# RWKV attention and a SoLU MLP on one core: v of the second half rounded by its own load, issued on GpSimd

## The chip, the core and the metric

The kernel runs on one core of one Trainium2 chip. The core's engines are PE (TensorE: matrix products and transposes), DVE (VectorE), ACT (ScalarE), POOL (GpSimd) and SP (SyncE, which here only issues transfers); 16 DMA engines move data between memory and the core's buffers. The metric is device time in microseconds (us), the median of several runs.

## What is computed

For 4 batches, 8 heads, 768 steps and heads of 48 numbers, a recurrence with a decaying state; the result is laid out as 3072 rows of 384 and goes through an MLP with a softmax gate and a normalization. Cut to what matters:

```python
for t in range(S):
    cur = np.einsum('bhd,bhe->bhde', u[None] * kt, vt)
    y[:, :, t] = np.einsum('bhd,bhde->bhe', rt, state + cur)
    state = wt[:, :, :, None] * state + np.einsum('bhd,bhe->bhde', kt, vt)
...
h = x @ w_in
e = np.exp(h - h_max)
solu = h * (e / np.sum(e))
ln = (solu - mean) / np.sqrt(var + 1e-06) * g_ln
out = ln @ w_out
```

r, k, v and w come in float32 as (batch, head, step, 48).

## The kernel before

The work is cut into 24 units: 6 chunks of 128 steps by 4 batches; unit i is chunk i // 4 of batch i % 4. In a unit the 128 steps lie on the 128 partitions and the 8 heads of 48 numbers side by side. Each unit passes through some forty small stages. The order of all stages of all units is one long string of words, `ORDER` (lines 21 to 66), that a loop at the end reads from left to right (lines 555 to 558): the word `vb12.p` calls the stage `vb` for unit 12 with the choice `p`. Each engine takes its own instructions strictly in that order (class `InOrder`, lines 71 to 89; this is why the profile gives line 85 for nearly all of them, and why groups are told apart by their tiles). An engine that has to wait for one instruction holds back all that it has behind it. Choices behind the dot are an engine (`a` ACT, `d` DVE, `p` POOL, `t` a transpose by DMA) or a bank of the PE's accumulators.

The stages that the change and the steps of the prediction touch:

- Loads `LW`, `LK`, `LR`, `LV` (lines 245 to 255): SP issues one transfer each for w, k, r and v of a unit. A unit's tile is 128 partitions by 8 heads by 48 numbers; in memory each run of 48 float32 stands alone, so a transfer is 1024 pieces of 192 bytes, 192 KB in all. The targets are rings of NIO = 7 tiles.
- `vb` (`v_cast`, line 355): a copy of v from float32 to bf16, on ACT, DVE or POOL as the word says, into one of NLW = 10 tiles `vb_t`.
- `p`, `q`, `qh` (POOL), `dg` (DVE), `dv` (`bonus_v`, POOL): the bonus term. p is r times k, q is p times u, `qh` adds the halves of q for some units, dg sums over a head, and dv is `vb` times dg.
- `S` (PE, line 433): the state's update, which reads kp and `vb`. `Y` (PE, line 405): the attention output, which reads the masked scores m and `vb`. `y` (ACT or DVE) brings it out; on DVE it adds dv.
- `M`, `m`, `sel`: the scores, their copy out (with the mask, on DVE; without it, on ACT) and the mask on POOL for those copied by ACT.
- The MLP: `X`, `xT` (transpose of y, two units by DMA), `H` (PE), `e` (ACT), `he` (DVE), `ea` (POOL, for 16 units, adds the halves of e), `hq` (ACT or DVE), `Oa`, `Ob` (PE), `sq`, `lv` (ACT), `qm` (DVE), `o` (ACT or DVE) and `out` (a store issued by SP).

The casts of v of units 12 to 23 stand on POOL for units 12, 13, 15, 16, 17, 18, 21 and 23, on DVE for 14, and on ACT for 19, 20 and 22. The word `LV` of these units stands 1 to 24 words before its `vb`.

SP has an in-order queue too. A load there waits until the tile that it overwrites has been read, and each transfer waits for the one eight before it to have landed.

Of the kernel before, what the change touches and what calls it, by code (L numbers as in the profile page):

```python
# [34 lines left out]
ex10 Oa2.3 st4 kr7.d dg7 LR9 LK9 kp9 X5.7 xT5.a LR10 Ob2 sq2 p9 q9 LK10 kp10 p10 cum11.6 ex11 qm2 lv2 o2.a S7.2  # L35
M7.4 m7.d H5.0 LK11 LR11 kp11 et7 st7 e5 he5 hq5.d dv7 out1 out3 LV9 vb9.d krk10.3 krr10 kr10.a p11 q11 Y7.n5
y7.d krk11.4 H6.6 ea5.p e6 M10.2 krr11 m10.a ea6.p qh9 LW12 lw12 krk9.1 krr9 LK12 LW15 lw15 kr9.d Oa5.0 X7.5
xT7.a he6 LR12 p12 out2 LK15 Ob5 sq5 dg9 q12 q10 qh12 kr11.d LR15 LV8 S9.1 et9 vb8.p sel10 st9 qm5 cum15.2 ex15
kp15 hq6.a cum12.6 ex12 kp12 H7.4 e7 he7 Oa4.1 LV12 qh11 vb12.p LV10 vb10.p LV11 dv8 M9.2 m9.a vb11.p sel9 Ob4
sq4 qm4 lv5 S8.7 hq7.d et8 st8 LW14 krk12.6 krr12 dg10 Y8.n3 y8.d kr12.a Oa6.2 lv4 o5.a M11.4 m11.a dg12 M12.6  # L40
m12.d Ob6 sq6 qm6 S10.0 et10 st10 S12.3 lv6 X8.5 xT8.d LK13 dv10 Y10.n4 y10.d o4.d et12 LW13 lw13 lw14 o6.a st12
S11.7 et11 st11 LR14 LR13 Oa7.6 LK14 dg11 LV13 cum13.4 ex13 kp13 cum14.0 ex14 kp14 H8.2 e8 dv12 Y12.i7 y12.a
X10.5 xT10.d dv9 p15 Y9.i4 y9.a sel11 LW18 lw18 LW16 krk14.1 krr14 vb13.p S13.0 et13 he8 lw16 dv11 p13 q13 hq8.a
LK16 H10.4 e10 X12.7 kr14.d M14.2 m14.a LW17 lw17 xT12.d dg13 X9.1 xT9.d st13 Y11.n7 y11.d p14 q14 Ob7 cum16.0
ex16 cum18.2 ex18 sq7 Oa8.7 he10 LR16 p16 q16 hq10.a kp16 qm7 lv7 X11.5 ea10.p sel14 LR18 LK18 kp18 Ob8 sq8
xT11.d qm8 cum17.0 ex17 krk13.4 krr13 o7.a kr13.d qh14 out4 LR17 LK17 kp17 H9.2 lv8 M13.4 m13.d LV16 e9 krk16.6
krr16 kr16.a H11.0 e11 q15 dg14 qh15 vb16.p S16.5 Oa10.4 LV14 vb14.d dv14 S14.6 o8.d he9 he11 krk17.7 krr17
kr17.d et16 Ob10 sq10 qm10 et14 hq9.a lv10 out5 out6 LV15 dv13 ea11.p p18 p17 LK19 st16 dg15 st14 out7 LW19 lw19
H12.2 e12 Y13.n1 Y14.n0 M17.6 y13.d X13.5 xT13.a o10.d Oa9.1 y14.d m17.a vb15.p q18 ea12.p cum19.4 ex19 Ob9 sq9
dg16 he12 qm9 lv9 q17 o9.a LR19 kp19 p19 dv15 sel17 X14.0 xT14.d H13.6 e13 M16.2 dv16 q19 qh19 m16.a sel16  # L50
hq11.d kr15.t M15.4 m15.d he13 H14.0 e14 ea13.p hq12.a LW20 lw20 qh18 ea14.p Oa11.5 kr18.t LV17 Y15.n4 y15.d
Ob11 he14 hq13.a sq11 out8 out10 M18.2 S15.7 et15 dg17 vb17.p LV18 out9 qm11 lv11 X15.6 xT15.a LR20 m18.d Oa12.4
cum20.0 ex20 st15 Ob12 sq12 qm12 Y16.n6 y16.d H15.2 o11.a LK20 LW21 kp20 vb18.p p20 dg18 dv18 dv17 X16.7 xT16.d
lv12 o12.d Y17.n5 e15 he15 lw21 hq14.a dg19 S17.6 et17 st17 y17.d H16.0 e16 q20 Y18.n7 Oa14.4 cum21.2 LW22 lw22
ex21 Ob14 sq14 y18.d he16 X18.6 xT18.a Oa13.5 kr19.t M19.0 LR21 LK21 ea15.p p21 q21 ea16.p hq16.a hq15.a kr20.t
kp21 LR22 m19.d M20.6 m20.d out12 H18.2 e18 ea18.p he18 LK22 p22 q22 Ob13 cum22.0 X17.7 xT17.a sq13 qm13 qm14
Oa16.6 ex22 kp22 LW23 lw23 lv13 o13.d hq18.d S18.7 et18 st18 dg20 LV19 vb19.a LK23 Ob16 sq16 qm16 dv19 LR23 LV20
lv14 o14.a H17.2 e17 he17 Oa15.1 cum23.4 ex23 ea17.p vb20.a dv20 qh21 Oa18.0 lv16 o16.a p23 q23 kp23 Y19.n7
y19.d Ob18 sq18 hq17.a Ob15 sq15 Y20.n3 y20.d X19.2 xT19.a kr21.t M21.4 m21.a sel21 dg22 dg21 qm18 kr22.t M22.6
m22.d qm15 S19.3 Oa17.2 et19 st19 LV22 vb22.a dv22 H19.4 out14 out11 lv18 o18.d lv15 o15.a Y22.n7 e19 Ob17 sq17  # L60
y22.d X22.6 dg23 qm17 lv17 xT22.a out13 o17.a he19 hq19.a LV21 vb21.p dv21 Y21.n3 xT20.t H20.0 e20 y21.d ea19.p
kr23.t M23.6 m23.d H22.4 e22 he20 hq20.a Oa19.2 LV23 vb23.p dv23 Y23.n3 y23.d out18 out16 he22 xT21.t H21.6 e21
X23.1 ea20.p hq22.d Ob19 sq19 xT23.a qm19 out17 he21 out15 lv19 o19.a out19 Oa20.0 hq21.d H23.4 e23 ea22.p Ob20
sq20 qm20 lv20 he23 hq23.d o20.a out20 ea21.p Oa21.3 Oa22.1 Ob21 sq21 qm21 lv21 Ob22 sq22 o21.a out21 qm22 lv22
o22.d out22 ea23.p Oa23.7 Ob23 sq23 qm23 lv23 o23.a out23
"""

NIO, NLW, NKP, NWK = 7, 10, 6, 4
# [24 lines left out]
def kernel(  # L93
# [25 lines left out]
    pe, act, dve, pool, sp = (InOrder(tc, e) for e in (nc.tensor, nc.scalar, nc.vector, nc.gpsimd, nc.sync))  # L119
# [6 lines left out]
    def ring(name, n, shape, dtype):  # L126
        return [consts.tile(shape, dtype, name=f"{name}{j}") for j in range(n)]
# [69 lines left out]
    vb_t = ring("vb", NLW, [C, H, D], BF16)  # L197
# [43 lines left out]
    def rows_of(src, i):  # L241
        c, b = units[i]
        return src[b, :, c * C:(c + 1) * C, :].rearrange("h t d -> t h d")
# [101 lines left out]
    def bonus_half(i, x):  # L345
        q = q_t[i % 3]
        pool.tensor_add(out=q[:, :, :D // 2], in0=q[:, :, :D // 2], in1=q[:, :, D // 2:])

    def v_cast(i, x):
        copy = {"a": act.copy, "d": dve.tensor_copy, "p": pool.tensor_copy}[x]  # L350
        copy(out=vb_t[i % NLW], in_=v_t[i % NIO][:, :, :D])
# [189 lines left out]
    def store(i, x):  # L541
# [4 lines left out]
        ih=make_halves, ik=make_keep, LW=load_w, LK=load_k, LR=load_r, LV=load_v, LU=load_u, LG=load_g, LI=load_w_in, LO=load_w_out,  # L546
        us=spread_u, uc=copy_u, gs=turn_g, gc=copy_g, wi=cast_w_in, gw=gain, mn=column_mean, mc=copy_mean,
        ce=centre, hot=warm_up,
        lw=log_w, cum=cumulate, ex=decays, kp=scaled, p=bonus_rk, q=bonus_u, vb=v_cast, dg=bonus_sum, qh=bonus_half, dv=bonus_v,
        krk=transposed_k, krr=transposed_r, kr=transposed_copy, M=scores, m=scores_copy, sel=scores_mask,  # L550
        Y=attend, y=y_copy, S=state, et=state_decay, st=state_update, X=x_transposed, xT=x_copy,
        H=hidden, e=hidden_exp, he=hidden_mul, ea=hidden_add, hq=hidden_square, Oa=output_a, Ob=output_b,
# [36 lines left out]
```

## Time and profile before

| | |
|---|---|
| median of 3 runs | 151.62 us (149.74 to 153.84) |
| the profiled execution | 152.17 us; its span 150.4 us |
| busy PE / DVE / ACT / POOL | 134.1 / 121.4 / 120.6 / 117.6 us |
| transfers of SP's queue | 113026 packets, 28.79 MB, 88.1% of the time of 16 DMA engines |
| loads of v | 24 of 192 KB, 3.8 us from issue to landing at the median |
| casts of v | 18 on POOL (9.4 us), 3 on DVE (1.4 us), 3 on ACT (1.5 us) |
| granted clock of PE | 1.0 |

The span is the time from the first to the last instruction of the profiled execution. A line of groups reads: source line, engine, operation, written tile `<-` read tiles, partitions x numbers and type, how many, then busy us and mean ns of one, then the idle time of the engine just before them and what ended it. A line of waits reads: who waited for whom, us in total, how many times, the longest. A line of the chain of work that ended last reads: start, length, engine and tile.

### The profile page before, as it was taken

To read this page: it belongs to the slowest core of one execution; us is meant where nothing else is said; L and a number is where in the kernel's file an instruction comes from. 1 tells how busy PE (TensorE), PEld (TensorE's weight loads), DVE (VectorE), ACT (ScalarE), POOL (GpSimd) and SP (SyncE) were. 2 spreads that over 40 slices of the span, in tenths; PEclk is the share of its full clock that TensorE was granted. 3 is DMA by queue.
4 is the path that set the end of the run, shared out by engine and by line. 5 is a ranking of instruction groups with operands and counts; after the bars stand their busy time and mean duration, and the time that the engine had idled before them with its cause. 6 is when DMAs were issued, how large, how long until landed. Compare 5 with 4: busy or idle time off the path is not lost.

```text
span 150.4 us, 5113 instructions
## 1 busy us (share of the span) xinstructions
PE 134.1 (89%) x2047; PEld 101.9 (68%) x2047; DVE 121.4 (81%) x216; ACT 120.6 (80%) x245; POOL 117.6 (78%) x152
## 2 busy tenths in 40 slices
PE   6967779788989999999999999989999999979960
PEld 2323548486667779777797889777977878868630
DVE  5025985799978999978997999999998989796620
ACT  3159588989987997999699995998898999986670
POOL 7339794897959999699989999999996989693300
PEclk9999999999999999999999999999999999999999
DMA  4999999599989999997999998998999996850131
GB/s 99 215 214 196 293 386 316 106 221 210 192 159 245 183 256 197 219 220 152 195 203 202 228 264 187 171 236 190 193 153 263 153 242 156 192 170 0 57 144 68
DMA packets 113051, 29.11 MB, mean 194 GB/s; under 512 B 108538, under 2 KB 112643, under 8 KB 113027
## 3 DMA queue, kind: packets, MB, share of 16 engines
q1 hardware_dynamic: 113026, 28.79, 88.1%
q8 instruction: 16, 0.26, 0.7%
q14 instruction: 9, 0.07, 0.2%
HBM read 22.03 MB, written 4.72 MB: 178 GB/s over the span
## 4 chain that ended last, share of the span: by engine, by line
PE 32%; POOL 13%; DVE 13%; DMA 12%; SPq 11%; ACT 11%; issue 5%; POOLq 0%
PE ps L85 32%; SPq L85 11%; DMA wout_f<-in_moe_w_out_dram 7%; POOL q L85 3%; DVE he L85 3%; POOL dv L85 3%; DMA xT<-y 3%; POOL p L85 3%; DMA kr_in<-in_r_dram 3%; POOL m L85 2%; DVE w L85 2%; POOL vb L85 2%; DVE kp L85 2%; ACT o L85 2%; DVE m L85 2%
## 5 line engine op out<-in xcount | busy, mean ns | idle before, releaser
L85 PE MATMUL ps<-w,he 128*128 128x385 bf16 x192 | 44.4, 324 | 0.5 <-DVE m L85 0.5
L85 PE MATMUL ps<-xT,win_sb 128*128 128x128 bf16 x576 | 36.0, 219 | 1.1 <-DMA xT<-y 1.1
L85 PEld LDWEIGHTS <-win_sb 128*128 128x128 bf16 x576 | 32.7, 98 | 2.7 <-issue 1.2
L85 PE MATMUL ps<-one_col,hq 128*128 128x1 bf16 x192 | 31.5, 164 | 0.0
L85 DVE TENSOR_TENSOR he<-ps,e 128x1024 bf16<-128x1024 f32 x24 | 29.1, 1218 | 0.6 <-ACT e L85 0.4
L85 DVE TENSOR_TENSOR kp<-ps,kr_in 128x768 bf16<-128x768 f32 x24 | 22.5, 951 | 8.4 <-ACT ps L85 7.5
L85 POOL TENSOR_TENSOR p<-kr_in 128x384 bf16<-128x384 f32 x24 | 24.0, 1001 | 6.0 <-DMA kr_in<-in_r_dram 5.0
L85 ACT ACTIVATE e<-ps 128x1024 bf16<-128x1024 f32 x24 | 24.5, 1019 | 5.1 <-PE ps L85 4.3
L85 POOL TENSOR_TENSOR ea<-e 128x512 bf16<-128x512 bf16 x16 | 18.4, 1154 | 7.3 <-ACT sq L85 4.2
L85 POOL TENSOR_TENSOR dv<-vb,dg 128x384 bf16<-128x384 bf16 x24 | 20.8, 876 | 2.7 <-DVE qm L85 1.7
L85 POOL TENSOR_TENSOR q<-p,u_bc 128x384 bf16<-128x384 bf16 x24 | 21.8, 912 | 1.2
L85 PEld LDWEIGHTS <-hq 128*128 128x128 bf16 x192 | 15.6, 96 | 8.5
L85 PEld LDWEIGHTS <-he 128*128 128x128 bf16 x192 | 18.4, 96 | 3.4
L85 ACT ACTIVATE ps<-ps 128x768 f32<-128x768 f32 x24 | 18.9, 800 | 0.7 <-PE ps L85 0.7
L85 DVE TENSOR_TENSOR m<-ps,keep 128x1024 bf16<-128x1024 f32 x14 | 17.0, 1218 | 1.3 <-PE ps L85 1.3
L85 PEld LDWEIGHTS <-kp 128*128 128x128 bf16 x216 | 13.1, 97 | 4.3 <-DVE kp L85 1.8
L85 ACT ACTIVATE hq<-he 128x1024 bf16<-128x1024 bf16 x15 | 15.7, 1055 | 0.1
L85 ACT ACTIVATE lw<-w_in 128x384 bf16<-128x384 f32 x23 | 11.8, 522 | 1.8 <-DMA w_in<-in_w_dram 1.8
L85 DVE TENSOR_REDUCE dg<-q 128x8 f32<-128x384 bf16 (+1 forms) x24 | 10.8, 453 | 2.2 <-POOL q L85 2.2
L85 PEld LDWEIGHTS <-kr 64*128 64x128 bf16 (+1 forms) x272 | 10.1, 95 | 3.6 <-ACT kr L85 1.2
L85 PE MATMUL ps<-ident,kp 128*128 128x128 bf16 x136 | 10.5, 220 | 1.7 <-DVE kp L85 1.2
L85 POOL CAST vb<-v_in 128x384 bf16<-128x384 f32 x18 | 9.4, 531 | 3.0 <-DMA v_in<-in_v_dram 3.0
(88 smaller groups left out, 289.8 us busy)
## 6 DMA issues: line engine op xcount, KB each, us to landing
kr_in<-in_k_dram SPq DMA_DIRECT2D x24, 192.0 KB, 3.8
kr_in<-in_r_dram SPq DMA_DIRECT2D x24, 192.0 KB, 4.0
w_in<-in_w_dram SPq DMA_DIRECT2D x24, 192.0 KB, 3.7
v_in<-in_v_dram SPq DMA_DIRECT2D x24, 192.0 KB, 3.8
out_dram<-o SPq DMA_DIRECT2D x24, 192.0 KB, 3.0
win_f<-in_moe_w_in_dram SPq DMA_DIRECT2D x3, 512.0 KB, 5.9
wout_f<-in_moe_w_out_dram SPq DMA_DIRECT2D x2, 768.0 KB, 9.8
kr<-kp SPq DMA_TRANSPOSE x7, 4.1
```

Source lines behind the costliest of these rows:

```text
L85: made = make(*args, **kwargs)
```

## The change

For units 12 to 23 the SP load of v into a float32 tile and the cast into `vb_t` are gone. In their place a transfer issued on POOL writes `vb_t` directly; it reads float32 and rounds to bf16 on the way. 24 words leave `ORDER` (`LV12` to `LV23` and `vb12` to `vb23`) and 12 come (`VB12` to `VB23`); all others keep their order. On POOL the twelve stand in this way (by the profile before, the place in front of each ends at the time in parentheses):

- `VB12` behind qh of unit 12 (66.6 us), `VB13` behind the mask of unit 9 (72.4)
- `VB16`, `VB14` behind q of unit 13 (80.4), `VB15` behind qh of unit 15 (88.6)
- `VB18` behind dv of unit 16 (101.3), `VB17` behind q of unit 19 (102.2), `VB19`, `VB20` behind q of unit 20 (110.9)
- `VB22` behind q of unit 22 (119.5), `VB21` behind qh of unit 21 (123.7), `VB23` behind q of unit 23 (125.7)

From each, 54 to 57 words of `ORDER` lie before the first stage that reads that tile. They wait for nothing else than their place: the tile was last used ten units earlier.

```diff
-xT7.a he6 LR12 p12 out2 LK15 Ob5 sq5 dg9 q12 q10 qh12 kr11.d LR15 LV8 S9.1 et9 vb8.p sel10 st9 qm5 cum15.2 ex15
-kp15 hq6.a cum12.6 ex12 kp12 H7.4 e7 he7 Oa4.1 LV12 qh11 vb12.p LV10 vb10.p LV11 dv8 M9.2 m9.a vb11.p sel9 Ob4
+xT7.a he6 LR12 p12 out2 LK15 Ob5 sq5 dg9 q12 q10 qh12 kr11.d LR15 LV8 VB12 S9.1 et9 vb8.p sel10 st9 qm5 cum15.2
+ex15 kp15 hq6.a cum12.6 ex12 kp12 H7.4 e7 he7 Oa4.1 qh11 LV10 vb10.p LV11 dv8 M9.2 m9.a vb11.p sel9 Ob4 sq4 qm4
...
+    def load_v_rounded(i, x):
+        pool.dma_start(out=vb_t[i % NLW], in_=rows_of(v, i))
+
     def v_cast(i, x):
         copy = {"a": act.copy, "d": dve.tensor_copy, "p": pool.tensor_copy}[x]
         copy(out=vb_t[i % NLW], in_=v_t[i % NIO][:, :, :D])
...
-        lw=log_w, cum=cumulate, ex=decays, kp=scaled, p=bonus_rk, q=bonus_u, vb=v_cast, dg=bonus_sum, qh=bonus_half, dv=bonus_v,
+        lw=log_w, cum=cumulate, ex=decays, kp=scaled, p=bonus_rk, q=bonus_u, vb=v_cast, VB=load_v_rounded, dg=bonus_sum, qh=bonus_half, dv=bonus_v,
```

More of the change, by code (lines that the diff above doesn't have):

```diff
@@ L37 @@
 y7.d krk11.4 H6.6 ea5.p e6 M10.2 krr11 m10.a ea6.p qh9 LW12 lw12 krk9.1 krr9 LK12 LW15 lw15 kr9.d Oa5.0 X7.5
-xT7.a he6 LR12 p12 out2 LK15 Ob5 sq5 dg9 q12 q10 qh12 kr11.d LR15 LV8 S9.1 et9 vb8.p sel10 st9 qm5 cum15.2 ex15
-kp15 hq6.a cum12.6 ex12 kp12 H7.4 e7 he7 Oa4.1 LV12 qh11 vb12.p LV10 vb10.p LV11 dv8 M9.2 m9.a vb11.p sel9 Ob4
-sq4 qm4 lv5 S8.7 hq7.d et8 st8 LW14 krk12.6 krr12 dg10 Y8.n3 y8.d kr12.a Oa6.2 lv4 o5.a M11.4 m11.a dg12 M12.6
+xT7.a he6 LR12 p12 out2 LK15 Ob5 sq5 dg9 q12 q10 qh12 kr11.d LR15 LV8 VB12 S9.1 et9 vb8.p sel10 st9 qm5 cum15.2
@@ L41 @@
+ex15 kp15 hq6.a cum12.6 ex12 kp12 H7.4 e7 he7 Oa4.1 qh11 LV10 vb10.p LV11 dv8 M9.2 m9.a vb11.p sel9 Ob4 sq4 qm4
+lv5 S8.7 hq7.d et8 st8 LW14 krk12.6 krr12 dg10 Y8.n3 y8.d kr12.a Oa6.2 lv4 o5.a M11.4 m11.a VB13 dg12 M12.6
 m12.d Ob6 sq6 qm6 S10.0 et10 st10 S12.3 lv6 X8.5 xT8.d LK13 dv10 Y10.n4 y10.d o4.d et12 LW13 lw13 lw14 o6.a st12
-S11.7 et11 st11 LR14 LR13 Oa7.6 LK14 dg11 LV13 cum13.4 ex13 kp13 cum14.0 ex14 kp14 H8.2 e8 dv12 Y12.i7 y12.a
-X10.5 xT10.d dv9 p15 Y9.i4 y9.a sel11 LW18 lw18 LW16 krk14.1 krr14 vb13.p S13.0 et13 he8 lw16 dv11 p13 q13 hq8.a
@@ L44 @@
-LK16 H10.4 e10 X12.7 kr14.d M14.2 m14.a LW17 lw17 xT12.d dg13 X9.1 xT9.d st13 Y11.n7 y11.d p14 q14 Ob7 cum16.0
+S11.7 et11 st11 LR14 LR13 Oa7.6 LK14 dg11 cum13.4 ex13 kp13 cum14.0 ex14 kp14 H8.2 e8 dv12 Y12.i7 y12.a X10.5
+xT10.d dv9 p15 Y9.i4 y9.a sel11 LW18 lw18 LW16 krk14.1 krr14 S13.0 et13 he8 lw16 dv11 p13 q13 hq8.a LK16 H10.4
+e10 X12.7 kr14.d M14.2 m14.a LW17 lw17 xT12.d dg13 X9.1 xT9.d VB16 st13 Y11.n7 VB14 y11.d p14 q14 Ob7 cum16.0
 ex16 cum18.2 ex18 sq7 Oa8.7 he10 LR16 p16 q16 hq10.a kp16 qm7 lv7 X11.5 ea10.p sel14 LR18 LK18 kp18 Ob8 sq8
-xT11.d qm8 cum17.0 ex17 krk13.4 krr13 o7.a kr13.d qh14 out4 LR17 LK17 kp17 H9.2 lv8 M13.4 m13.d LV16 e9 krk16.6
@@ L47 @@
[L47 to L65, printed above, removed]
+xT11.d qm8 cum17.0 ex17 krk13.4 krr13 o7.a kr13.d qh14 out4 LR17 LK17 kp17 H9.2 lv8 M13.4 m13.d e9 krk16.6 krr16
@@ new lines @@
+kr16.a H11.0 e11 q15 dg14 qh15 S16.5 Oa10.4 VB15 dv14 S14.6 o8.d he9 he11 krk17.7 krr17 kr17.d et16 Ob10 sq10
+qm10 et14 hq9.a lv10 out5 out6 dv13 ea11.p p18 p17 LK19 st16 dg15 st14 out7 LW19 lw19 H12.2 e12 Y13.n1 Y14.n0
+M17.6 y13.d X13.5 xT13.a o10.d Oa9.1 y14.d m17.a q18 ea12.p cum19.4 ex19 Ob9 sq9 dg16 he12 qm9 lv9 q17 o9.a LR19
+kp19 p19 dv15 sel17 X14.0 xT14.d H13.6 e13 M16.2 dv16 VB18 q19 VB17 qh19 m16.a sel16 hq11.d kr15.t M15.4 m15.d
+he13 H14.0 e14 ea13.p hq12.a LW20 lw20 qh18 ea14.p Oa11.5 kr18.t Y15.n4 y15.d Ob11 he14 hq13.a sq11 out8 out10
@@ new lines @@
+M18.2 S15.7 et15 dg17 out9 qm11 lv11 X15.6 xT15.a LR20 m18.d Oa12.4 cum20.0 ex20 st15 Ob12 sq12 qm12 Y16.n6
+y16.d H15.2 o11.a LK20 LW21 kp20 p20 dg18 dv18 dv17 X16.7 xT16.d lv12 o12.d Y17.n5 e15 he15 lw21 hq14.a dg19
+S17.6 et17 st17 y17.d H16.0 e16 q20 Y18.n7 Oa14.4 cum21.2 LW22 lw22 VB19 ex21 Ob14 sq14 y18.d he16 X18.6 xT18.a
+Oa13.5 kr19.t M19.0 LR21 VB20 LK21 ea15.p p21 q21 ea16.p hq16.a hq15.a kr20.t kp21 LR22 m19.d M20.6 m20.d out12
+H18.2 e18 ea18.p he18 LK22 p22 q22 Ob13 cum22.0 X17.7 xT17.a sq13 qm13 qm14 Oa16.6 ex22 kp22 LW23 lw23 lv13
@@ new lines @@
+o13.d VB22 hq18.d S18.7 et18 st18 dg20 LK23 Ob16 sq16 qm16 dv19 LR23 lv14 o14.a H17.2 e17 he17 Oa15.1 cum23.4
+ex23 ea17.p dv20 qh21 VB21 Oa18.0 lv16 o16.a p23 q23 kp23 Y19.n7 y19.d Ob18 sq18 hq17.a Ob15 sq15 Y20.n3 VB23
+y20.d X19.2 xT19.a kr21.t M21.4 m21.a sel21 dg22 dg21 qm18 kr22.t M22.6 m22.d qm15 S19.3 Oa17.2 et19 st19 dv22
+H19.4 out14 out11 lv18 o18.d lv15 o15.a Y22.n7 e19 Ob17 sq17 y22.d X22.6 dg23 qm17 lv17 xT22.a out13 o17.a he19
+hq19.a dv21 Y21.n3 xT20.t H20.0 e20 y21.d ea19.p kr23.t M23.6 m23.d H22.4 e22 he20 hq20.a Oa19.2 dv23 Y23.n3
@@ L66 @@
+y23.d out18 out16 he22 xT21.t H21.6 e21 X23.1 ea20.p hq22.d Ob19 sq19 xT23.a qm19 out17 he21 out15 lv19 o19.a
+out19 Oa20.0 hq21.d H23.4 e23 ea22.p Ob20 sq20 qm20 lv20 he23 hq23.d o20.a out20 ea21.p Oa21.3 Oa22.1 Ob21 sq21
+qm21 lv21 Ob22 sq22 o21.a out21 qm22 lv22 o22.d out22 ea23.p Oa23.7 Ob23 sq23 qm23 lv23 o23.a out23
 """
```

## The prediction

> **What bounds the kernel now.** I read the page first: busy times, the 40 slices, the chain that ended last. No engine is far ahead of the others (PE 89%, DVE 81%, ACT 80%, POOL 78%), so the shares decide nothing, and I went to the stretch in which the change lies: from the end of unit 12's halving on GpSimd (66.5 us) to the last bonus product before the tail (131 us).
>
> Busy time by stretch (length, then PE, PEld, DVE, ACT, POOL, each with its count; granted clock, DMA share, GB/s):
>
> ```profile
> 66.50:131.00 64.50, 63.80 (x1099) 52.12 (x1094) 60.63 (x103) 57.74 (x126) 60.22 (x71) 1.00 0.99 197
> 131.00:150.40 19.40, 13.04 (x195) 10.00 (x188) 9.89 (x15) 11.14 (x26) 5.85 (x6) 1.00 0.27 96
> ```
>
> In the first row POOL works 60.22 of 64.50 us: 4.28 us are free. PE shows 63.80, but its records run into one another, so this is no proof that PE is full. The transfers are in flight all the time (0.99), yet hardly anything waits for them, as the next view shows. All of GpSimd's waits in this stretch:
>
> ```profile
> POOL ea L85 <- ACT e L85: 1.8, 2, 1.3
> POOL vb L85 <- DMA v_in<-in_v_dram: 0.5, 1, 0.5
> POOL dv L85 <- DVE vb L85: 0.3, 1, 0.3
> POOL m L85 <- ACT et L85: 0.2, 1, 0.2
> ```
>
> That is 2.8 us (the other 1.5 are short gaps between instructions). v costs 0.8 of it in waits. What GpSimd does there, by form:
>
> ```profile
> L85 POOL TENSOR_TENSOR dv<-vb,dg 128x384 bf16<-128x384 bf16 x15 | 12.7, 860 | 0.4 <-DVE vb L85 0.3
> L85 POOL TENSOR_TENSOR ea<-e 128x512 bf16<-128x512 bf16 x10 | 11.5, 1155 | 1.8 <-ACT e L85 1.8
> L85 POOL TENSOR_SCALAR_AFFINE_SELECT m<-m 128x1024 bf16<-128x1024 bf16 x7 | 8.1, 1157 | 0.2 <-ACT et L85 0.2
> L85 POOL CAST vb<-v_in 128x384 bf16<-128x384 f32 x10 | 5.4, 553 | 0.5 <-DMA v_in<-in_v_dram 0.5
> L85 POOL TENSOR_TENSOR q<-q 128x192 bf16<-128x192 bf16 x7 | 3.8, 547 | 0.2
> ```
>
> The chain that ended last is on GpSimd before and after this stretch and passes through it by other engines (PE, ACT, DVE). Its last crossing of GpSimd leads straight into the tail:
>
> ```profile
> 125.91 0.49 POOL m L85
> 126.40 0.55 issue
> 126.95 0.83 POOL dv L85
> 127.78 0.46 POOL vb L85
> 128.24 0.07 issue
> 128.31 0.83 POOL dv L85
> 129.14 1.12 POOL ea L85
> 130.26 0.05 issue
> 130.31 0.56 DVE y L85
> 130.89 3.95 DMA xT<-y
> ```
>
> What makes GpSimd late before 129 us makes y of unit 21, its transpose, and the last hidden layers late. So the change is priced on GpSimd.
>
> **What goes.** Of the ten POOL casts in the stretch, seven belong to units 12, 13, 15, 16, 17, 18 and 21; units 8, 10 and 11 keep theirs, at 0.50 each. 5.53 (ten at 553 ns) less 1.50 is 4.03 us. Unit 23's cast (0.50, at 131.7, after a wait of 1.42 for its v) lies behind the chain's crossing and counts nothing. DVE loses one cast (unit 14, 0.68 us at 88.6) and ACT three (19, 20, 22: 0.50, 0.50, 0.52). These two engines have 3.9 and 6.8 us free in the stretch, against POOL's 4.3, so nothing is counted while POOL is the later one; that cover goes only if the new issues are nearly free (third and fourth rivals). SP loses 12 of its issues. Their row, and who waits for v:
>
> ```profile
> L85 SPq DMA_DIRECT2D v_in<-in_v_dram x24: 413/720/5322, 10.1 to 128.5; - x24
> DMA to landing us min/median/max: 3.1/3.8/10.3
> ```
>
> Twelve at 0.72 are 8.6 us of SP's queue. What comes behind moves up: r, k and w loads, transposes by DMA, stores. But no p, kp or lw in the stretch waits for a load (the four waits above are all of POOL's; DVE and ACT show none for a transfer), and the transposes sent by SP wait for y or kp, not for their place in the queue. I count nothing. The order of every other instruction stays.
>
> **What comes.** Twelve transfers are issued on GpSimd, all between 66.6 us (behind unit 12's halving) and about 126 us (behind unit 23's q). They need no new wait: their buffer is the one of ten units earlier, long read. Behind each stands GpSimd's queue in order: masks of m (PE's attend waits), dv (DVE's or ACT's y waits), ea (PE's output waits), p and q (DVE's dg). Where one instruction is late, all behind it are.
>
> The transfer itself: v is wanted by the first of dv, S or Y, more than 50 words later in the written order; for unit 12 S and dv come about 6.5 us after the issue point, for unit 21 about 4.6 us plus the delay that the new issues bring. A v load lands 3.8 us after its issue at the median. I count no wait. The 1024 pieces per transfer are the same, so the load on the DMA engines is counted unchanged.
>
> The unknown is how long one issue holds GpSimd; no transfer in this trace is issued there. Bounds from rows:
> - Below: GpSimd's shortest instruction in the page's groups by form, a memset of 2x8, takes 0.09 us. SP's shortest issue of the same load is 0.41, its median 0.72.
> - Above: SP's longest issue of it, 5.32, with the DMA engines full. And if GpSimd works out 1024 pieces at the pace of its small product (192 numbers per partition in 547 ns, 2.85 ns each), 1024 x 2.85 = 2.92, plus 0.41 for the sending: 3.33.
> - Taken: the nearest GpSimd row that makes 1024 items from a counted pattern is the mask of m, 128x1024 in 1.14 us over the whole span (11.3 us in 10). With 0.41 for the sending that is 1.55 us.
>
> **The sum.** 12 x 1.55 = 18.6. Less the casts, 4.0; less the waits of 2.8 that a later GpSimd swallows (what it waited for is ready by then): +11.8 us. The profiled execution took 152.17 (span 150.4 plus 1.8 around it), the median of three is 151.62. I put the sum on the median: 163.4 us; on the profiled execution it would be 164.0. With c for one issue, the change is 12c - 6.8, so GpSimd alone breaks even at c = 0.57.
>
> One rule speaks against my price. The Trainium skill (DMA: Bandwidth & Descriptors, section on the anatomy of a DMA on the SWDGE path) calls descriptor generation small and variable: many can be emitted before the added cost shows. By it the 1.14 would fall away, c would be 0.41, and the sum would be the second rival's, no change. This trace bears it out only for SP, whose stores of 128 rows take 0.53 us at the median and loads of 1024 pieces 0.72; SP is not GpSimd.
>
> **The rivals.**
>
> 1. *GpSimd's issue must give way to VectorE.* The trace shows the two in each other's way: unit 12's cast took 1.01 us instead of 0.50 while DVE ran hq at 68.56 us, and DVE's hq, 0.69 at the median, took 1.32 while a mask of m ran 1.56. If each issue loses the longest common DVE instruction, 1.22 us (he, m), c is 2.77 and the time 151.6 + 33.2 - 6.8 = 178.0. Against it: most of GpSimd's rows are steady beside a VectorE busy 94% of the stretch. The Trainium skill (SBUF — State Buffer, section on the wrong bandwidth-pool intuition) has a GpSimd-issued DMA go from about 620 ns alone to about 3100 ns beside a VectorE copy; twelve at that figure would give an estimate of 151.6 + 37.2 - 6.8 = 182, and no row here shows such an issue.
>
> 2. *An issue costs GpSimd about what it costs SP.* c between 0.41 and 0.72: 12c is 4.9 to 8.6, against 4.0 of casts and 2.8 of waits; -1.9 to +1.8 on GpSimd, and below zero the other full engines hold the end. 151.6. For it: on SP the number of pieces hardly shows. Against: SP only hands on, GpSimd would have to work the addresses out.
>
> 3. *The other side: GpSimd is hardly held, and the casts are a gain.* At c = 0.09, 4.0 of casts and 0.8 of waits for v go, 1.1 comes: 3.7 us, 147.9, if nothing else takes over. It decides below c = 0.15 (4.8 - 12c over 3.0, which is 2%). Against: three other engines are at 57.7 to 63.8 of 64.5 us, and GpSimd has no instruction of real size near 0.1.
>
> 4. *An issue stalls like SP's longest*, because the DMA engines are full (0.99) and the queue must drain before it takes 1024 pieces: c = 5.32, 63.8 - 6.8, 208.6 us. For it: SP has issues of 2 to 5 us. Against: its median is 0.72, under the same load.
>
> **The numbers.** My forecast (c from 0.72 to 3.33, 153.4 to 184.8) has 0.50; rival 1 has 0.12, rival 2 0.16, rival 3 0.10, rival 4 0.12. The range 149 to 186 leaves out rival 4 and most of rival 3, 0.20 in all. Within the forecast alone I expect 157 to 175 (c 1.0 to 2.5). A measurement of this kernel tells about 2%, 3.0 us, from no change. Slower by more: 0.48 of the forecast, rivals 1 and 4: 0.72. Within: rival 2, 0.02 of the forecast, 0.02 of rival 3: 0.20. Faster: 0.08.
>
> **What would show it.** In the profile after: twelve issues in GpSimd's queue; their duration against 1.55 is the test of the whole sum. Right, if p, q, dv and ea behind an issue start late by it, the chain through 66 to 130 us lies on GpSimd and its queue, and dv21's start moves from 128.3 to about 140. PE should show new waits for m, dv or ea. Rival 1: issue times spread widely, long ones beside DVE's hq and copies. Rival 2 or 3: issues under 0.7, the chain still on PE and ACT. I am wrong in kind if GpSimd computes on while its transfers are prepared, if v lands late and dv or S waits for it, or if other loads slow down because two queues now share the DMA engines.

## The result and the profile after

The changed kernel takes 157.38 us (median of 4 runs, 156.84 to 158.10), the kernel before beside it 152.38 (149.74 to 153.84): ratio 1.043, 95% interval [1.037, 1.048], slower. The forecast was 163.4 us in a range of 149 to 186. The side came out as forecast, and the mechanism in the main; the size, +11.8 us, was more than twice what was measured. On two other chips, where before took about 155 us, the ratio was 1.025 [1.016, 1.035] and 1.025 [1.019, 1.030]. Times are medians of all runs of a kernel; the ratios leave out the runs that fell in a slower state.

The profiled execution has a span of 155.6 us. The twelve issues are in GpSimd's queue. Here is their row among the instructions that read v (name, count, nanoseconds min/median/max, first and last start), with the time to landing; the latter holds SyncE's twelve loads too:

```profile
L84 SPq DMA_DIRECT2D v_in<-in_v_dram x12: 454/705/4356, 10.1 to 63.0; - x12
L84 POOL DMA_DIRECT2D vb<-in_v_dram x12: 881/937/1114, 64.8 to 131.0; - x12
DMA to landing us min/median/max: 3.4/4.8/9.6
```

An issue holds GpSimd for 0.94 us, not 1.55, and all twelve are alike. The DMA part of the page of the profile gives the new transfers alone:

```profile
vb<-in_v_dram POOLq DMA_DIRECT2D x12, 96.0 KB, 5.4
```

They land later than SyncE's loads of k and r (5.4 against 3.8 us at the median). Nothing waits for them in this profile, but in both later profiles of the changed kernel PE waits once, 0.6 and 0.9 us, for the v of unit 17. The loads of k, r and w do not suffer (3.8, 3.8 and 3.5 us here, 3.8, 4.0 and 3.7 before); SyncE's seven transposes of kp land in 5.2 us instead of 4.1. GpSimd's groups from the first issue (64.8 us) to 137 us:

```profile
L84 POOL TENSOR_TENSOR dv<-vb,dg 128x384 bf16<-128x384 bf16 x16 | 13.0, 828 | 3.1 <-DVE dg L84 3.0
...
L84 POOL DMA_DIRECT2D vb<-in_v_dram x12 | 11.3, 943 | 0.0
...
L84 POOL CAST vb<-v_in 128x384 bf16<-128x384 f32 x3 | 1.5, 499 | 0.0
```

11.3 us came, and 4.0 of casts went (5.5 to 1.5): 7.3 us more. The stretch from the first issue's place to the end of ea of unit 19 was 66.5 to 130.3 us and is now 64.8 to 135.8: 7.2 us longer. (GpSimd reached its first issue 1.7 us earlier than it had reached this place before; that place lies at 64.8, 66.6 and 67.7 us in three profiles of the changed kernel, so 1.7 us are within what one kernel varies by.) So the whole of the 7.3 shows here, though 2.8 us of waits were to be swallowed. They did go, but one wait took their place. (In the two later profiles the stretch is 5.4 and 5.5 us longer.) All of GpSimd's waits from the first issue on, while the stretch lasts:

```profile
POOL dv L84 <- DVE dg L84: 3.0, 1, 3.0
```

Its reason is on the chain that ended last (start, length, engine and tile):

```profile
70.78 21.60 PE ps L84 x364
...
98.73 3.80 DVE hq L84
102.53 1.14 DVE m L84
...
103.71 25.03 PE ps L84 x382
```

VectorE's square hq of unit 11, which took 1.32 us before and 0.69 when nothing is in its way, took 3.88. Behind it m came late and PE stood still for 3.0 us, whose work between 100 and 110 us is down from 9.54 to 6.98, at a granted clock of 0.83 (0.61 from 104 to 106 and 0.54 from 106 to 108, right behind the standstill; 1.00 over the same ten in the kernel before; busy us of PE, PEld, DVE, ACT and POOL, then clock, DMA share, GB/s):

```profile
100.00:110.00 10.00, 6.98 (x87) 4.74 (x85) 8.60 (x9) 5.73 (x11) 9.43 (x11) 0.83 1.22 172
```

hq of unit 7 was held back too, 3.56 us from 66.70.

In this profile, then, the chain between 66.5 and 131 us lies on PE and passes through hq; it does not lie on GpSimd, which was the prediction's sign of being right. The two later profiles of the changed kernel show it there (us of the chain in that window):

| profile | PE | GpSimd |
|---|---|---|
| before | 34.9 | 8.5 |
| the change, first | 47.4 | 0.0 |
| the change, second and third (experiment 3) | 11.7, 0.0 | 36.4, 51.7 |
| no transfers, no casts (experiment 1) | 46.4 | 3.8 |
| memsets in place of the issues (experiment 2) | 4.5 | 47.9 |

The crossing of GpSimd into the tail answers to the one of before:

```profile
131.96 0.75 POOL m L84
132.71 0.31 issue
133.02 0.85 POOL dv L84
133.89 0.56 DVE y L84
...
136.02 0.56 DVE y L84
136.59 4.10 DMA xT<-y
```

The transpose of y that opens the tail starts at 136.59 instead of 130.89.

### The profile page after: what moved, and what is told of

Read it like the earlier page. It is cut to its first block, busy times and chain, and to the rows that moved or that the text cites. A ratio compares the mean times of both kernels' runs of the same rounds, so it can differ in the third digit from the quotient of the medians.

```text
span 155.6 us, 5103 instructions
## 1 busy us (share of the span) xinstructions
PE 135.1 (87%) x2045; PEld 102.5 (66%) x2047; DVE 126.2 (81%) x215; ACT 120.2 (77%) x242; POOL 124.1 (80%) x156
## 3 DMA queue, kind: packets, MB, share of 16 engines
q0 software_dynamic: 12480, 1.18, 14.4%
## 4 chain that ended last, share of the span: by engine, by line
PE 38%; SPq 18%; DVE 16%; ACT 8%; POOL 8%; DMA 5%; issue 5%; DVEq 0%
PE ps L84 38%; SPq L84 18%; POOL q L84 4%; DVE hq L84 3%; DMA xT<-y 3%; DVE he L84 2%; DMA kr_in<-in_k_dram 2%; DVE kp L84 2%; POOL p L84 2%; DVE m L84 2%; ACT o L84 1%; DVE y L84 1%; DVE dg L84 1%; ACT lv L84 1%; POOL dv L84 1%
## 5 line engine op out<-in xcount | busy, mean ns | idle before, releaser
L84 PE MATMUL ps<-w,he 128*128 128x385 bf16 x192 | 45.2, 328 | 3.0 <-DVE m L84 3.0
L84 POOL TENSOR_TENSOR dv<-vb,dg 128x384 bf16<-128x384 bf16 x24 | 20.3, 858 | 4.4 <-DVE dg L84 3.3
L84 POOL TENSOR_TENSOR q<-p,u_bc 128x384 bf16<-128x384 bf16 x24 | 22.1, 922 | 1.1
L84 PEld LDWEIGHTS <-kr 64*128 64x128 bf16 (+1 forms) x272 | 10.5, 96 | 5.8 <-issue 3.0
L84 ACT ACTIVATE lw<-w_in 128x384 bf16<-128x384 f32 x23 | 11.8, 522 | 1.5 <-DMA w_in<-in_w_dram 1.5
L84 DVE TENSOR_TENSOR hq<-he 128x1024 bf16<-128x1024 bf16 x9 | 12.6, 1395 | 0.1
L84 DVE TENSOR_TENSOR y<-ps,dv 128x384 bf16<-128x384 f32 x18 | 9.7, 551 | 3.5 <-PE ps L84 1.7
```

The costliest lines, as they stand in the source:

```text
L84: made = make(*args, **kwargs)
```

## The experiments

Three theories. A: the issues hold GpSimd, and that is the loss. B: the held time is mostly covered, and the loss is VectorE's two squares. C: the new transfers disturb the others. Every ratio is to the kernel before on the same chip; each is known to about 0.6% to either side, so two ratios less than 1% apart are hardly told apart.

**1. No transfers and no casts.** The words `LV12` to `LV23` and `vb12` to `vb23` are left out of the kernel before.

> The kernel before without the loads and casts of v of units 12 to 23; their products use what the buffers still hold, so v of these units is left out. This is the change at no price for its transfers. Theory A (the twelve issues hold GpSimd for 12 x 0.94 = 11.3 us, against 4.0 us of casts and some waits): without them GpSimd is 4 to 5 us less loaded than before, ratio to before 0.97 to 0.985. Theory B (the issues are mostly covered, the loss is VectorE's square hq held back twice for 3 us behind GpSimd): casts are then as well covered, ratio 0.99 to 1.0. Theory C (the new transfers disturb the other transfers): as B.

152.36 us against 154.83: ratio 0.989 [0.982, 0.995]. Taking 4.0 us of casts and all waits for v away gains 1.8 us (1.15% of 154.8): casts and loads of v were covered by more than half. The ratio lies between the ranges of A (0.97 to 0.985) and B (0.99 to 1.0). With the other stages in this order, it also bounds what another way of loading these v could win.

**2. The held time without a transfer.**

```diff
-        pool.dma_start(out=vb_t[i % NLW], in_=rows_of(v, i))
+        pool.memset(hold, 0.0)
```

> The changed kernel with each of the twelve issues replaced by a GpSimd memset of 128x930 bf16 (about 0.94 us, as the issue) into a spare buffer; no transfer, v of units 12 to 23 is left out. Theory A: the held time is all that counts, ratio to before 1.03 to 1.045, as with the change. Theory B: near the change as well if the phase of GpSimd against VectorE stays, 1.0 to 1.04, to be read from the durations of hq. Theory C: without transfers no loss, 1.0 to 1.01.

156.39 us: ratio 1.013 [1.007, 1.019]. The memsets lasted as long as the issues, nearly:

```profile
L84 POOL MEMSET hold<- x12: 865/876/884, 67.5 to 130.0; 128x930 bf16 x12
```

hq stayed under 1.2 us. The ratio is below A's range and above C's: without any transfer there is a loss, so C does not make all of it. It is smaller than that of the change, so something is left for B or C.

**3. The squares of units 7 and 11 on ScalarE**, in both kernels (`hq7.d hq11.d` become `hq7.a hq11.a`).

> The kernel before with the squares hq of units 7 and 11 moved to ScalarE, the measure for the run with the same move in the changed kernel. Both theories: within 1% of before, since hq took 0.69 and 1.32 us there and ScalarE has 6.8 us free in the stretch from 66.5 to 131 us for two squares of 1.06.

154.41 us: ratio 0.998 [0.994, 1.003]. The move alone changes nothing that shows.

> The changed kernel with the squares hq of units 7 and 11, which took 3.6 and 3.9 us on VectorE instead of 0.69, moved to ScalarE (1.06 us each). Theory A: the loss against the kernel before with the same move stays at 3 to 4%. Theory B: it falls to 0 to 1.5%, this kernel 3 to 5 us faster than the change.

156.66 us: ratio 1.013 [1.006, 1.020], as B said. The changed kernel itself had not run on this chip, so the two were run side by side:

> The changed kernel once more, so that it stands beside the other runs on one chip. Theory B (about 1.3% of the loss is the time that GpSimd is held, the rest is VectorE's square hq of units 7 and 11 held back): ratio to before 1.03 to 1.045, hq again over 3 us twice in its profile. Theory A (held time alone): ratio about 1.013, as with the memsets in place of the issues, and the long hq of the first profile was a chance of that execution.

159.19 us: ratio 1.025 [1.016, 1.035]. That is between the two; hq of unit 7 was over 3 us again, hq of unit 11 was not.

> The changed kernel with hq of units 7 and 11 on ScalarE again, beside the changed kernel itself. Theory B: 2 to 3% faster than it. Theory A: within 1% of it.

156.80 us: ratio 1.021 [1.014, 1.027]. By the ratios it is 0.5% faster, as A said.

> The changed kernel a third time, to pair with the next run. If VectorE's held-back squares cost it time beside the held GpSimd, it is 1 to 2% slower than the next; if not, within 0.5%.

158.88 us: ratio 1.025 [1.019, 1.030].

> The changed kernel with hq of units 7 and 11 on ScalarE, a third time: ratio to before 1.013 to 1.02, as the two times before; 1 to 2% faster than the changed kernel if the squares count.

156.61 us: ratio 1.009 [1.006, 1.013]. The move of the two squares makes the changed kernel 0.5% faster in the first pair, where the intervals overlap widely, and 1.5% in the second, where they are apart. Over three runs its loss is 1.3, 2.1 and 0.9%, against 2.5% and 2.5% for the change on two of these chips. So of the change's loss of 2.5%, some 1.4 points stay without the squares, and about 1 point is the squares; one pair of two shows that clear of noise. Neither A nor B alone is right; held time and squares together fit best, though the range given for that (1.03 to 1.045, with two long squares) was missed.

hq of unit 7 was long in all three profiles of the changed kernel (3.56, 3.04, 3.06 us); hq of unit 11 only in the first (3.88, then 1.07 and 1.07). How it is held back is seen by setting GpSimd and VectorE side by side (start, length, instruction). The kernel before:

```profile
68.05 0.55 POOL L85 TENSOR_TENSOR q<-q 128x192 bf16<-128x192 bf16 x1
68.61 1.46 POOL L85 CAST vb<-v_in 128x384 bf16<-128x384 f32 x2
70.03 0.82 POOL L85 TENSOR_TENSOR dv<-vb,dg 128x384 bf16<-128x384 bf16 x1
...
68.56 0.69 DVE L85 TENSOR_TENSOR hq<-he 128x1024 bf16<-128x1024 bf16 x1
```

The changed kernel, its second profile:

```profile
66.56 1.11 POOL L84 DMA_DIRECT2D vb<-in_v_dram  x1
67.69 0.51 POOL L84 CAST vb<-v_in 128x384 bf16<-128x384 f32 x1
68.16 1.09 POOL L84 TENSOR_SCALAR_AFFINE_SELECT m<-m 128x1024 bf16<-128x1024 bf16 x1
69.22 0.54 POOL L84 TENSOR_TENSOR q<-q 128x192 bf16<-128x192 bf16 x1
69.71 0.49 POOL L84 CAST vb<-v_in 128x384 bf16<-128x384 f32 x1
70.18 0.82 POOL L84 TENSOR_TENSOR dv<-vb,dg 128x384 bf16<-128x384 bf16 x1
70.95 0.49 POOL L84 CAST vb<-v_in 128x384 bf16<-128x384 f32 x1
71.41 1.53 POOL L84 TENSOR_SCALAR_AFFINE_SELECT m<-m 128x1024 bf16<-128x1024 bf16 x1
...
68.95 3.04 DVE L84 TENSOR_TENSOR hq<-he 128x1024 bf16<-128x1024 bf16 x1
```

hq multiplies he by itself, so both its inputs lie in SBUF, the core's buffer memory. It is the only one of VectorE's products that stretches: he, m, kp, y and st, with one input in the accumulators, stay within 3% of their medians in the profile of before and in the first one of the change. Before, hq started as GpSimd changed instructions; it ran its 0.69 us, and GpSimd's cast waited (the two casts take 1.46 instead of 1.00). In the changed kernel hq starts while the mask of m runs, and GpSimd's next four instructions get in ahead of it one after the other at full speed; only the second mask is held up (1.53 instead of 1.09), and hq ends in it. With the memsets, and with transfers of 128 pieces, hq also began during that mask and got its turn right behind it (0.93 and 1.18 us, and GpSimd's next q 0.98 and 0.97 instead of 0.54).

**4. The issue alone moved.** GpSimd issues the same loads in float32 into the old buffers, and the casts stay.

```diff
+    def load_v_pool(i, x):
+        pool.dma_start(out=v_t[i % NIO][:, :, :D], in_=rows_of(v, i))
```

> The issue alone is moved: at the same places GpSimd issues the loads of v of units 12 to 23 in float32 into the old buffers, and the casts stay where they were before. Theory A: 11.3 us more of GpSimd than before instead of 7.3, so 1 to 2% slower than the change. Theory B: the same held time, 0.5 to 1% on top of the change if hq is held back as there, but 1.02 to 1.03 to before if it is not. If rounding on the way makes the packets slow, their time per packet (28.7 ns in the change, 19.4 in the queue of SyncE) falls here to that of SyncE's.

160.61 us: ratio 1.044 [1.035, 1.053], 1.8% above the change beside it, as A said. An issue takes 0.94 us here too, so rounding adds nothing on GpSimd; it saves the casts, and makes the packets small. hq of unit 7 took 1.78 us: one instruction of GpSimd got in ahead of it, and then GpSimd had nothing to do for 1.4 us. The queue rows of this run and of the change (packets, MB, share of 16 engines' span):

```profile
q0 software_dynamic: 768, 2.36, 5.8%
```

```profile
q0 software_dynamic: 12480, 1.18, 14.4%
```

The expectation compared times per packet; since the packets themselves are others (64 for a load here, 1040 in the change), that comparison says nothing on rounding.

**5. Fewer pieces.** Each transfer takes 128 long rows of the weights in place of v.

```diff
-        pool.dma_start(out=vb_t[i % NLW], in_=rows_of(v, i))
+        pool.dma_start(out=vb_t[i % NLW].rearrange("t h d -> t (h d)"), in_=moe_w_in[:128, :DM])
```

> The changed kernel with each of the twelve transfers taking 128 rows of 384 numbers of the weights w_in (128 pieces of 1536 bytes, rounded on the way) in place of v in 1024 pieces; v of units 12 to 23 is left out. If GpSimd's time for an issue is made of its pieces, as the prediction had it (0.41 for the sending and 1.14 for 1024 pieces), an issue falls from 0.94 to about 0.5 us and the ratio to before to about 1.0. If it is a fixed time, it stays at 0.85 to 0.95 us and the ratio at 1.01 to 1.025; what the ratio then falls by is what the 1024 small packets cost the other transfers.

```profile
L84 POOL DMA_DIRECT2D vb<-in_moe_w_in_dram x12: 537/593/772, 66.4 to 127.2; - x12
```

154.24 us: ratio 1.002 [0.996, 1.007]. The issue falls from 0.94 to 0.59 us for 896 pieces less. If the time grows evenly with the pieces, which two points cannot show, that is 0.39 ns a piece, and 0.54 us that do not depend on them. Time and ratio are near what was expected for an issue made of its pieces, but two thirds of the prediction's 1.14 us for them are not there.

**6. Twelve issues more.** A second issue behind each, of the same v, into one spare buffer.

> The changed kernel with a second issue behind each of the twelve, of the same v into a spare buffer: 11.3 us more of GpSimd and the same transfers once more. Theory A: if GpSimd is the bound by now, nearly all of it shows, ratio to before 1.09 to 1.12. Theory B (only about a third of the held time reached the end with the memsets): the change's ratio and 0.025 more, 1.05 to 1.07, unless hq is held longer still. Theory C (the transfers disturb the others): also longer landing of k, r and w, and waits for them.

181.83 us against 154.90: ratio 1.182 [1.172, 1.192]. That is above the ranges of A and B. This run says little on the issues: its page of the profile shows GpSimd waiting 14.7 us for the spare buffer's last transfer to land. A spare buffer for each of the twelve does not fit into SBUF beside the others (213.5 KB per partition are wanted, 207.9 are left). With four spare buffers in turn, and the two squares on ScalarE:

> The changed kernel with hq of units 7 and 11 on ScalarE and with a second issue behind each of the twelve, of the same v, into four spare buffers in turn, so that an issue waits only for the landing of the one four before. GpSimd has 11.3 us more than in the run with the move of hq alone (there +7.3 against before, ratio 1.009 to 1.021). Runs without held-back squares lie on a line so far: -4.0 us of GpSimd 0.9885, +3.2 us (the issues of 128 pieces) 1.0017, +6.5 us (memsets) 1.0127, +7.3 us 1.014, about 0.35 us at the end for each us. If the line goes on, +18.6 us gives 1.035 to 1.045. If GpSimd becomes the bound, as the prediction had it (12c less 6.8, all beyond shows), it gives 1.014 and 0.073 more, 1.08 to 1.095. If the transfers or their landing hold it, above 1.12.

166.36 us against 153.00 (1.087 by the medians; no interval, since the runs of before beside it spread from 148.98 to 153.61). That is in the range named for GpSimd as the bound, 1.08 to 1.095. There is no wait for a spare buffer now, and GpSimd is full. Busy us of PE, PEld, DVE, ACT and POOL:

```profile
66.50:138.00 71.50, 64.28 (x1037) 51.93 (x1034) 55.30 (x94) 55.46 (x118) 70.38 (x81) 0.95 1.36 167
```

70.38 of 71.50 us. PE waited once for a new v here, 1.9 us. The run with the squares moved alone took 156.6 to 156.8 us on other chips; 10.7 us of second issues (12 at 0.89) made it about 10 longer. Beyond the point at which GpSimd has no idle time left, nearly each microsecond shows, as the prediction had it.

**What the runs say together**, by GpSimd's work in the stretch against before:

| run | GpSimd, us | ratio |
|---|---|---|
| no transfers, no casts | -4.0 | 0.989 |
| issues of 128 pieces (7.2 - 4.0) | +3.2 | 1.002 |
| memsets (10.5 - 4.0) | +6.5 | 1.013 |
| the change, squares on ScalarE (11.3 - 4.0) | +7.3 | 1.009 to 1.021 |
| the change | +7.3 | 1.025, 1.025, 1.043 |
| issue moved, casts kept | +11.2 | 1.044 |
| two issues, squares on ScalarE (22.1 - 4.0) | +18.1 | 1.087 |

From -4.0 to +3.2 the end moves 0.28 us for each of GpSimd's (0.0132 x 155 / 7.2), from +3.2 to +6.5 half a microsecond, from +6.5 to +18.1 one (0.074 x 154 / 11.6). The first two slopes have errors of some 0.2 and 0.4 us, since each ratio is known to about 0.6%; that a microsecond costs more at the end of the table than at its start is safe, where it turns is not. The memsets, which move no data, lose as much as the change with its squares moved, so the transfers themselves cost nothing that shows beyond this 0.6%, though PE waited once for a v in four of the six profiles of these two kernels; theory C falls as a main cause. The change alone lies above the curve, and comes down towards it with the two squares moved.

## Why the prediction was right, and where it was off

- *What bounds.* Right in the main: the loss comes with GpSimd's work, in the stretch that was named, and showed at the crossing into the tail (dv of unit 21 at about 133.8 us instead of 128.3; about 140 was said, for an issue of 1.55). The sign that the chain lies on GpSimd came in two profiles of three; in the first it lay on PE, which had waited for m behind the held-back square. No rival and no term of the sum had VectorE as the one that is held.
- *What goes.* The casts were 4.0 us, as worked out. The relief of SP, DVE and ACT was not tested by itself; together with GpSimd's 4.0 us it gains 1.8 us, so it cannot count for much. That no v lands late, which was counted as no wait, did not quite hold: PE waited 0.6 to 1.2 us for the v of unit 17 in four profiles of six.
- *The price of an issue.* This is the step that was mis-sized: 1.55 us taken, 0.94 measured. Of its two parts the sending was 0.54 (0.41 taken) and the 1024 pieces 0.40 (1.14 taken): GpSimd does not write out pieces at the pace of its masks. The rule of the Trainium skill (DMA: Bandwidth & Descriptors, the anatomy of a DMA on the SWDGE path) that generation is small and many can be emitted before it shows was nearer for the pieces than the row: 0.39 ns a piece. It is not nothing, though: 0.59 against 0.94 us was 4.2 us over twelve issues, and these two kernels stand 4.6 us apart on one chip (154.24 and 158.88), squares included.
- *12c less 6.8.* With c = 0.94 it gives 11.3 - 6.8 = +4.5 us, close to the 5.0 between the medians on the first chip; on the two others the loss was 2.5%, 3.9 us. That is luck in part, as two errors met. The 2.8 us of waits were swallowed, but a new one of 3.0 took their place in the first profile; and without the held-back squares the loss is about 1.4% or 2.2 us, since up to some +6 us of GpSimd's work a part is covered by the other engines. That all beyond 6.8 us shows, as was said, holds only from there on (0.28, 0.5, then 1).
- *Rival 1, issue against VectorE.* The other way round. The issues were steady (0.88 to 1.12 us), where the estimate by the Trainium skill (SBUF — State Buffer, the wrong bandwidth-pool intuition) had 3.1 us each; no run here shows an issue held. That section of the Trainium skill gives the 3100 ns for a whole DMA, so it was no price for the time that an issue holds GpSimd. It was VectorE that lost, with an instruction that reads SBUF twice.
- *Rivals 2 to 4.* Rival 2's price for an issue (0.41 to 0.72) holds for 128 pieces, and there its result came, 1.002. Rival 3 falls: GpSimd is held. Rival 4 falls: no issue was above 1.12 us.
- *Open.* Why hq is passed over at GpSimd's changes of instructions in some executions and gets its turn at the first one in others is not settled. An issue right ahead of it does not decide it: hq of unit 11 was passed over in the first profile, by a mask, a dv and an issue, though the last issue before it had ended 8.6 us earlier; behind the same instructions it got its turn at once in the second and third profile (1.07 us); and with two issues in a row ahead (the first run of experiment 6) hq of unit 7 took only 0.94.

## What to carry to other kernels

Moving a load to GpSimd to save a cast is an exchange on GpSimd's own queue: compare the issue (0.94 us for 1024 pieces, 0.59 for 128) with the cast that goes (0.50), before asking about the transfer. On a kernel with four nearly full engines, what is taken off one of them gains little (1.8 us here for 4.0 and the relief of three others) and what is added costs up to its whole length. Look also at the durations on other engines: here VectorE's one product that reads SBUF twice lost up to 3.2 us, several times its own length, behind a GpSimd queue without gaps. And take more than one profile: the first of this case had a chain and a second long square that the next two did not have.

## What the runs showed of the hardware that was not expected

- A load that rounds on the way goes in 1040 packets each (12480 in 12), and the same load from GpSimd without rounding in 64 (768 in 12). In time of the 16 DMA engines that is 29.9 us against 12.3 for one load (14.4% of 155.6 x 16 / 12; 5.8% of 158.6 x 16 / 12). It landed in 5.4 against 4.4 us. None of this cost time here that the ratios show; on a kernel bound by its transfers, which no run here is, it would be a thing to look at.
- GpSimd's time for an issue did not depend on the rounding (0.94 with and without).
- VectorE's square of 0.69 us took up to 3.88 us beside instructions of GpSimd of 0.5 to 1.1 us, of which only the last was slowed (1.53 instead of 1.09, 1.19 instead of 0.92).
